# Delta rule and cosine router: chunks of 64 tokens with two sequences to a tile, in place of chunks of 128

## The chip, the cores and the metric

The kernel runs on one core of a Trainium2 chip. TensorE (PE; PEld is its weight load) multiplies, VectorE (DVE), ScalarE (ACT) and GpSimd (POOL) work on what it makes, SyncE (SP) issues most transfers. The metric is the device time of one execution in microseconds, less is better.

## The reference

Four sequences, 8 heads, 768 tokens, head size 48, all in float32. A delta rule makes one output row a token; the rows (3072 of 384) go to a router that picks one of 8 experts by cosine similarity, and each expert is two matrix products with a ReLU between them.

```
k_n = k / (norm(k) + 1e-06)
for t in range(S):
    kt, vt, bt = k_n[:, :, t], v[:, :, t], beta[:, :, t, None]
    y[:, :, t] = einsum('bhd,bhde->bhe', q[:, :, t], state)
    v_old = einsum('bhde,bhd->bhe', state, kt)
    state = state + bt * einsum('bhd,bhe->bhde', kt, vt - v_old)
x = y.transpose(0, 2, 1, 3).reshape(B * S, H * D)
logits = (x / |x|) @ (emb / |emb|).T / tau          # argmax picks the expert, softmax gives the gate
out[mask] = gate_w[mask] * (maximum(x[mask] @ w1[e], 0) @ w2[e])
```

## The kernel before, in words

The tokens of a sequence are cut into chunks (NC = 6 of C = 128). Inside a chunk the loop over tokens becomes linear algebra: with A the strictly triangular part of beta-weighted K K^T, the new values are Z = (I + A)^-1 (V - K S), the outputs Q S + (Q K^T) Z, and the state grows by (beta K)^T Z. A tile holds the 128 tokens of one sequence; heads lie behind each other in the free dimension.

`prep` (L182) normalises K on POOL and DVE. `front` (L201) transposes K, Q and beta K on PE (L207, copied out by ACT, L208), makes K K^T and K Q^T of each head (L215; the 48 rows of a head at partition 0 or 64), masks them (L220 on DVE, L222 and L223 on ACT and POOL) and starts the inverse, W, on POOL (L228, L229). `invert` (L233) doubles the inverted blocks in six levels (`LEVELS` 2 to 64); each level of a group of four heads is four transposes (L240, copied by ACT, L242), four products (L248, masked by DVE, L251) and four more (L257, added by DVE, L260). Two sequences, so four groups, go through a level together. `back` (L262) then does for each sequence K S (L268, R on DVE, L271), the solve (L276, Z on ACT), Q S and the outputs (L284, L287), the state (L299, added by DVE, L303), the transposes of the output (L307) and its logits (L312). `route` (L315) runs once a chunk: small DVE instructions, two small products (L349) and four indirect writes of token numbers to `idmap` by POOL (L362).

The loop (L367) runs over 6 chunks and, in each, over 2 pairs of sequences. The order of the instructions on each engine is made by a scheduler from the program. PSUM has two rings of tiles, `big` (5) and `seq` (3). Behind the loop the second half runs over 31 tiles of 128 routed tokens: fetch of indices, rows and weights, three transposes (L443), 24 products (L453), 8 products (L458), and the result is written by index (L461). A float32 product is two instructions on PE (each row of the trace counts them so), a transpose is one.

Of the kernel before, what the change touches and what calls it, by code (L numbers as in the profile page):

```python
# [15 lines left out]
C = 128  # L16
T = 128
LEVELS = (2, 4, 8, 16, 32, 64)
# [3 lines left out]
def kernel(  # L22
# [37 lines left out]
    def big(shape):  # L60
        return ps.tile(shape, F32, name="big", tag="big", bufs=5)

    def seq(shape):
        return ps.tile(shape, F32, name="seq", tag="seq", bufs=3)
# [6 lines left out]
    half = cpool.tile([128, B, H], F32, name="half")  # L71
    nc.vector.memset(half, 0.5)
    mask_su = cpool.tile([128, 1, 128], F32, name="mask_su")
    nc.gpsimd.memset(mask_su, 1.0)
    nc.gpsimd.affine_select(out=mask_su, in_=mask_su, compare_op=ALU.is_ge, fill=0.0, base=-1,
                            pattern=[[0, 1], [1, 128]], channel_multiplier=-1)
# [28 lines left out]
    xor_i = ac.tile([128, 128], I32, name="xor_i")  # L105
    row_i = ac.tile([128, 128], I32, name="row_i")
    nc.gpsimd.iota(xor_i, pattern=[[1, 128]], base=0, channel_multiplier=0)
    nc.gpsimd.iota(row_i, pattern=[[0, 128]], base=0, channel_multiplier=1)
    nc.vector.tensor_tensor(xor_i, xor_i, row_i, op=ALU.bitwise_xor)
    xor_f = ac.tile([128, 128], F32, name="xor_f")  # L110
    nc.vector.tensor_copy(xor_f, xor_i)
    nmask1 = ac.tile([128, 1, 128], F32, name="nmask1")
    nc.vector.scalar_tensor_tensor(out=nmask1[:, 0, :], in0=xor_f, scalar=1.0, in1=mask_su[:, 0, :],
                                   op0=ALU.is_equal, op1=ALU.mult)
    nc.vector.tensor_scalar_mul(nmask1, nmask1, -1.0)
    nlow = ac.tile([128, 128], F32, name="nlow")
    nc.gpsimd.memset(nlow, -1.0)
    nc.gpsimd.affine_select(out=nlow, in_=nlow, compare_op=ALU.is_ge, fill=0.0, base=-1,
                            pattern=[[-1, 128]], channel_multiplier=1)
    nmask = {}  # L120
    for s in LEVELS:
        m = ac.tile([128, 1, 128], F32, name=f"nmask{s}")
        nc.vector.scalar_tensor_tensor(out=m[:, 0, :], in0=xor_f, scalar=float(s), in1=nlow,
                                       op0=ALU.is_ge, op1=ALU.mult)
        if 2 * s < C:
            nc.vector.scalar_tensor_tensor(out=m[:, 0, :], in0=xor_f, scalar=float(2 * s), in1=m[:, 0, :],
                                           op0=ALU.is_lt, op1=ALU.mult)
        nmask[s] = m


    Qp = []
    for i in range(2):
        t = ac.tile([128, B, H, 64], F32, name=f"Qp{i}")
        nc.gpsimd.memset(t, 0.0)
        Qp.append(t)
    KK = []
    for i in range(6):
        t = ac.tile([128, 2, H, 64], F32, name=f"KK{i}")
        nc.vector.memset(t, 0.0)
        KK.append(t)  # L140
    S_bd = ac.tile([128, B, NP, 2, D], F32, name="S_bd")
    nc.vector.memset(S_bd, 0.0)

    def load(c):
        K4 = io.tile([128, B, H, D], F32, name="K4", tag="K4")
        V4 = io.tile([128, B, H, D], F32, name="V4", tag="V4")
        for b in range(B):
            for dst, src in ((K4[:, b], k), (Qp[c % 2][:, b, :, 0:D], q), (V4[:, b], v)):
                nc.sync.dma_start(out=dst, in_=src[b, :, c * C:(c + 1) * C, :].rearrange("h p d -> p h d"))
        return K4, V4  # L150
# [7 lines left out]
    loaded = load(0)  # L158
# [345 lines left out]
```

## Time and profile before

| | us |
|---|---|
| median of 3 runs | 1604.41 (1603.41 to 1612.71) |
| profiled execution | 1606.1 |
| its span, first to last instruction | 1604.3 |
| PE busy | 1389.4 (87%) |
| DVE, ACT, POOL busy | 561.2, 309.6, 336.1 |
| mean granted clock of TensorE | 0.865 |

The page has the busy time of each engine, the span in 40 slices, the chain that ended last and the costliest groups of instructions. Waits are named by the engine and line that ended them. [...]

### The profile page before, as it was taken

Reading aid. Unit: us, or ns where it says so; the run is one execution under the profiler, and the core shown is the slowest. Engines: PE = TensorE matmul, PEld = TensorE weight load, DVE = VectorE, ACT = ScalarE, POOL = GpSimd, SP = SyncE. Lnnn points to the kernel's source line nnn. Section 1 sums busy time; section 2 is a strip of 40 time slices with the busy share of each in tenths; the row PEclk is TensorE's granted clock in tenths of the full one; section 3 lists DMA queues with packets and bytes.
Section 4 is the critical chain, followed back from the end, with each engine's and each line's share of the span. In section 5 each row is a group of like instructions: output and inputs, shape, how many; then the busy total and the mean of one; then the engine's idle time right before and its main releaser. Section 6 shows DMA issues by size and latency. Waiting matters only on the chain. (4 is left out here: it accounts for less than half of the span.)

```text
span 1604.3 us, 24107 instructions
## 1 busy us (share of the span) xinstructions
PE 1389.4 (87%) x10166; PEld 1275.2 (79%) x10166; DVE 561.2 (35%) x1001; ACT 309.6 (19%) x599; POOL 336.1 (21%) x316
## 2 busy tenths in 40 slices
PE   3698997989879898798988989799892799999997
PEld 2697987979779798797978979699792578878875
DVE  4451644426344263442634435253352001110110
ACT  2122221222212222112221132222220011111110
POOL 7803024030240302203031030400301111111110
PEclk9796978979779797897968999598895799999999
DMA  9100021000210002000010000000001999999991
GB/s 153 21 1 11 1 50 20 1 11 1 53 18 1 11 1 50 1 1 11 1 40 1 1 1 1 20 1 1 1 1 54 356 330 324 317 327 325 330 318 48
DMA packets 132349, 129.04 MB, mean 80 GB/s; under 512 B 82698, under 2 KB 117681, under 8 KB 132242
## 3 DMA queue, kind: packets, MB, share of 16 engines
q1 hardware_dynamic: 127298, 116.55, 24.3%
q0 software_dynamic: 4736, 10.85, 1.9%
q8 instruction: 80, 1.31, 0.3%
q14 instruction: 27, 0.22, 0.0%
q10 hardware_dynamic: 208, 0.11, 0.0%
HBM read 117.91 MB, written 10.95 MB: 80 GB/s over the span
## 5 line engine op out<-in xcount | busy, mean ns | idle before, releaser
L251 DVE TENSOR_TENSOR Pm<-big,nmask 128x512 f32<-128x512 f32 x288 | 198.2, 691 | 308.6 <-PE big L248 308.6
L248 PE MATMUL big<-Ti,LM 128*128 128x128 f32 x2304 | 292.1, 289 | 0.0
L248 PEld LDWEIGHTS big<-Ti,LM 128*128 128x128 f32 x2304 | 287.3, 206 | 0.0
L257 PE MATMUL big<-W,Pm 128*128 128x128 f32 x2304 | 269.5, 275 | 2.6 <-DVE Pm L251 2.6
L257 PEld LDWEIGHTS big<-W,Pm 128*128 128x128 f32 x2304 | 263.1, 192 | 3.2 <-DVE Pm L251 3.2
L242 ACT ACTIVATE Ti<-big 128x512 f32<-128x512 f32 x288 | 152.8, 600 | 562.9 <-PE big L240 562.9
L240 PE MATMUL big<-ident,W 128*128 128x128 f32 x1152 | 157.4, 287 | 111.5 <-POOL W L229 107.2
L240 PEld LDWEIGHTS big<-ident,W 128*128 128x128 f32 x1152 | 134.1, 147 | 126.1 <-POOL W L229 118.3
L260 DVE TENSOR_TENSOR W<-big,W 128x512 f32<-128x512 f32 x288 | 198.8, 692 | 56.4 <-PE big L257 56.2
L453 PE MATMUL big<-xTm,w 128*128 128x128 f32 x1488 | 173.1, 277 | 0.0
L453 PEld LDWEIGHTS big<-xTm,w 128*128 128x128 f32 x1488 | 170.7, 194 | 0.3
L458 PE MATMUL seq<-w,hT 128*128 128x384 f32 x496 | 165.1, 486 | 0.0
L196 POOL TENSOR_TENSOR KK<-KK,betaT 128x384 f32<-128x384 f32 x24 | 19.7, 827 | 594.8 <-PE seq L299 594.8
L458 PEld LDWEIGHTS seq<-w,hT 128*128 128x128 f32 x496 | 91.9, 190 | 57.5
L460 DVE TENSOR_SCALAR y<-seq,xg 128x384 f32<-128x384 f32 x31 | 19.1, 618 | 305.0 <-PE seq L458 305.0
L455 ACT ACTIVATE hT<-big 128x512 f32<-128x512 f32 x62 | 37.0, 598 | 336.4 <-PE big L453 291.3
L215 PE MATMUL big<-KT 48*128 48x256 f32 x384 | 71.1, 487 | 10.1 <-ACT KT L208 10.1
L287 PE MATMUL seq<-Z,LM 128*128 128x48 f32 x384 | 65.8, 341 | 2.3 <-ACT Z L279 2.3
L215 PEld LDWEIGHTS big<-KT 48*128 48x128 f32 x384 | 50.3, 235 | 21.4 <-ACT KT L208 14.8
L287 PEld LDWEIGHTS seq<-Z,LM 128*128 128x128 f32 x384 | 64.7, 262 | 2.9 <-ACT Z L279 2.9
L461 POOL DMA_INDIRECT out_dram<-y,ids x31 | 31.5, 1018 | 163.2 <-DVE y L460 159.8
L228 POOL TENSOR_TENSOR W<-LM,nmask 128x512 f32<-128x512 f32 x48 | 60.7, 1265 | 10.2 <-DVE LM L220 9.2
(131 smaller groups left out, 1026.4 us busy)
## 6 DMA issues: line engine op xcount, KB each, us to landing
w<-in_moe_w_dram SPq DMA_DIRECT2D x62, 1536.0 KB, 9.5
x_dram<-xc SPq DMA_DIRECT2D x6, 770.0 KB, 4.1
K<-in_k_dram SPq DMA_DIRECT2D x24, 192.0 KB, 4.0
V<-in_v_dram SPq DMA_DIRECT2D x24, 192.0 KB, 4.1
Qp<-in_q_dram SPq DMA_DIRECT2D x24, 192.0 KB, 3.1
ids<-idmap SPq DMA_DIRECT2D x31, 0.5 KB, 8.6
xg<-x_dram,ids POOLq DMA_INDIRECT x31, 6.9
out_dram<-y,ids POOLq DMA_INDIRECT x31, 7.1
```

The source lines that it names most:

```text
L215: nc.tensor.matmul(psG[:, i], lhsT=KT[pr, 2 * g + i, 2, :], rhs=KT[pr, 2 * g + i, 0:2, :], start=True, stop=True, skip_group_check=True)
L228: nc.gpsimd.tensor_tensor(W, LM[:, hh, :, 0, :], nmask1.broadcast_to([128, NP, 128]), op=ALU.mult)
L240: nc.tensor.transpose(psI[:, j, :], W[:, j, :], ident)
L242: nc.scalar.activation(Ti, psI, ACT.Copy)
L248: nc.tensor.matmul(psP[:, j, :], lhsT=AT[:, j, :], rhs=Ti[:, j, :], start=True, stop=True, skip_group_check=True)
L251: nc.vector.tensor_tensor(Pm, psP, nmask[s].broadcast_to([128, NP, 128]), op=ALU.mult)
L257: nc.tensor.matmul(psW[:, j, :], lhsT=Pm[:, j, :], rhs=W[:, j, :], start=True, stop=True, skip_group_check=True)
L260: nc.vector.tensor_tensor(Wn, psW, W, op=ALU.add)
L287: nc.tensor.matmul(psY[:, h, :], lhsT=LM[:, h % 2, h // 2, 1, :], rhs=Z[:, h, :], start=(c == 0 and h == 0), stop=True, skip_group_check=True)
L453: nc.tensor.matmul(psH[:, i, :], lhsT=w1[:, j, (f + i) * 128:(f + i + 1) * 128], rhs=xT[:, j, :], start=(j == 0), stop=(j == KC - 1))
L455: nc.scalar.activation(hT[:, f:f + 4, :], psH, ACT.Relu)
L458: nc.tensor.matmul(psO, lhsT=hT[:, f, :], rhs=w2[:, f, :], start=(f == 0), stop=(f == NF - 1))
```

## The change

Chunks are 64 tokens (NC = 12), and a tile holds the 64 tokens of two sequences, one in each half of the partitions (`HALF`); a chunk is therefore two tiles, u = 0 and 1, for the four sequences. Every product of the recurrence is a 64 by 64 tile of TensorE: rows from one half of the partitions, columns to one half. `products`, `of_state`, `state`, `base` and `grow` use all four places of the array in turn, and the two row halves write different PSUM banks; `x_plain`, `x_square`, `solve`, `lower`, `outputs` and `last` use two (both rows and both columns, on a diagonal). The transposes stay 128 by 128.

The inverse starts from blocks of 4 rows, (I + X)(I + X^2) with X the masked A (`x_plain`, `x_square`, `base`), and goes through four levels (4 to 32). It keeps T, the transpose of W, beside W: `grow` makes both from the same operands, so the transposes of the levels are gone, and `lower` multiplies with A masked for each level beforehand on POOL (`AN`, four a tile, with `XT` and `XTI` before them). beta is put into the mask (`MM`) on POOL, so beta K is not transposed. All PSUM tiles share one ring, `bank` (8).

The steps of `front(c+1)` and of `back(c)` alternate in the program, one step of `back` behind each second step of `front`; on PE that order is kept as written, the other engines are scheduled as before. `route` runs once in two chunks. The second half keeps its instructions. The diff, cut to its core (A is the strictly triangular part of LM):

```diff
-C = 128
+C = 64
 T = 128
-LEVELS = (2, 4, 8, 16, 32, 64)
+LEVELS = (4, 8, 16, 32)
...
-        return ps.tile(shape, F32, name="big", tag="big", bufs=5)
...
-        return ps.tile(shape, F32, name="seq", tag="seq", bufs=3)
...
+        return ps.tile(shape, F32, name="bank", tag="bank", bufs=8)
...
+            p, u = slice(b % 2 * C, b % 2 * C + C), b // 2
...
+    HALF = (slice(0, C), slice(C, 2 * C))
+
+    def mm(out, lhsT, rhs, start=True):
+        nc.tensor.matmul(out, lhsT=lhsT, rhs=rhs, start=start, stop=True, skip_group_check=True)
...
+            nc.gpsimd.tensor_tensor(MM[(c * NU + u) % len(MM)], upper.broadcast_to([128, H, C]),
+                                    betaT[:, c, u].unsqueeze(2).broadcast_to([128, H, C]), op=ALU.mult)
...
+    def front(c):
...
+        def transposes():
+            for u in us:
+                kk = KK[(c * NU + u) % len(KK)]
...
+                for i, src in enumerate((kk[:, 0], Qp[c % 2][:, u])):
+                    psT = bank([128, NP, 128])
+                    for j in range(NP):
+                        nc.tensor.transpose(psT[:, j, :], src[:, 2 * j:2 * j + 2, :].rearrange("p h d -> p (h d)"),
+                                            ident)
+                    nc.scalar.activation(KT[u][:, :, i, :], psT, ACT.Copy)
...
+        def products():
+            for u in us:
...
+                psG = [bank([128, NP, 2, C]) for _ in range(2)]
+                for j in range(NP):
+                    for jj in range(2):
+                        pr = slice(jj * C, jj * C + D)
+                        for i in range(2):
+                            mm(psG[jj][HALF[i], j], KT[u][pr, j, 0, HALF[i]], KT[u][pr, j, :, HALF[i]])
...
+                for jj in range(2):
+                    nc.vector.tensor_tensor(LM[u][:, jj], psG[jj],
+                                            mv[:, jj].unsqueeze(2).broadcast_to([128, NP, 2, C]), op=ALU.mult)
...
+                nc.gpsimd.tensor_tensor(XT[u], A, nmask[0].broadcast_to([128, H, C]), op=ALU.mult)
...
+                nc.gpsimd.tensor_tensor(XTI[u], XT[u], id64h, op=ALU.add)
+                for s in LEVELS:
...
+                    nc.gpsimd.tensor_tensor(AN[u, s], A, nmask[s].broadcast_to([128, H, C]), op=ALU.mult)
...
+        def x_plain():
+            for u in us:
+                p = bank([128, H, C])
+                for h in range(H):
+                    for i in range(2):
+                        mm(p[HALF[i], h], XT[u][HALF[i], h], id64[HALF[i], 0])
...
+                nc.scalar.activation(X[u], p, ACT.Copy)
...
+        def x_square():
...
+                        mm(p[HALF[i], h], XT[u][HALF[i], h], X[u][HALF[i], h])
...
+                nc.vector.tensor_tensor(X2[u], p, id64h, op=ALU.add)
...
+        def new_t(u, p):
...
+            nc.scalar.activation(T_[u], p, ACT.Copy)
...
+        def new_w(u, p):
...
+            nc.vector.tensor_copy(W[u], p)
...
+        def base():
...
+                pt, pw = bank([128, H, C]), bank([128, H, C])
+                for h in range(H):
+                    for i in range(2):
+                        mm(pt[HALF[i], h], XTI[u][HALF[i], h], X2[u][HALF[i], h])
+                        mm(pw[HALF[1 - i], h], X2[u][HALF[i], h], XTI[u][HALF[i], h])
+                new_t(u, pt)
+                new_w(u, pw)
...
+        def lower(s):
...
+                        mm(p[HALF[1 - i], h], AN[u, s][HALF[i], h], T_[u][HALF[i], h])
...
+                nc.vector.tensor_tensor(Pm[u], p, id64h, op=ALU.add)
...
+        def grow(s):
...
+                        o = HALF[1 - i]
+                        mm(pw[o, h], Pm[u][o, h], W[u][o, h])
+                        mm(pt[HALF[i], h], W[u][o, h], Pm[u][o, h])
+                new_t(u, pt)
+                new_w(u, pw)
...
+        def last():
...
+                        mm(p[HALF[i], h], Pm[u][o, h], W[u][o, h])
...
+                nc.scalar.activation(W[u], p, ACT.Copy)
...
+        steps = [transposes, products, x_plain, x_square, base]
+        for s in LEVELS[:-1]:
+            steps += [lambda s=s: lower(s), lambda s=s: grow(s)]
+        steps += [lambda: lower(LEVELS[-1]), last]
+        return steps, (KT, LM, W)
...
+        def of_state():
...
+                                mm(p[jj][HALF[i], u, j], KT[u][pr, j, a, HALF[i]], S_all[pr, u, j, i])
...
+                        nc.vector.tensor_tensor(dv, vv, p[jj], op=ALU.subtract)
...
+                        nc.scalar.activation(dv, p[jj], ACT.Copy)
...
+        def solve():
...
+                        mm(p[HALF[i], h], w[HALF[i]], r[HALF[i], u, h])
...
+                nc.scalar.activation(Z[u], p, ACT.Copy)
...
+        def state():
...
+                        mm(p[i][HALF[h % 2], u, h // 2], kb[HALF[i], h], Z[u][HALF[i], h])
+            for i in range(2):
+                nc.vector.tensor_tensor(S_all[:, :, :, i], p[i], S_all[:, :, :, i], op=ALU.add)
...
+        def outputs():
...
+                        mm(p[HALF[i], h], LM[u][HALF[i], h % 2, h // 2, 1], Z[u][HALF[i], h])
...
+                    nc.vector.tensor_tensor(xb, pf, Yq[0][:, u].rearrange("p h d -> p (h d)"), op=ALU.add)
...
+        def x_transposes():
...
+        def logits():
...
+        return [of_state, solve, state, outputs, x_transposes, logits]
...
+    with tc.manual_schedule(engines={mybir.EngineType.PE}):
+        prep(0, loaded[0][0])
+        loaded[1] = load(1)
+        steps, fr = front(0)
+        for f in steps:
+            f()
...
+        for c in range(NC):
...
+            if c + 2 < NC:
+                loaded[c + 2] = load(c + 2)
+            bs = back(c, fr, loaded.pop(c)[1], xc, ssx, lz)
+            if c + 1 < NC:
+                prep(c + 1, loaded[c + 1][0])
+                steps, fr = front(c + 1)
+                for i, f in enumerate(steps):
+                    f()
+                    if i % 2 == 1 and bs:
+                        bs.pop(0)()
+            for f in bs:
+                f()
+            if c % 2 == 1:
+                route(c, xc, ssx, lz)
```

On POOL, before, the front of a pair of sequences has for each of its four groups a select, a masking and an addition of the unit matrix:

```order
L223 AFFINE_SELECT LM<-LM 128x512
L228 TENSOR_TENSOR W<-LM,nmask_111 128x512
L229 TENSOR_TENSOR W<-W,ident 128x512
L223 AFFINE_SELECT LM<-LM 128x512
L194 TENSOR_TENSOR KK_144<-K_1650,rn 128x8x48
L228 TENSOR_TENSOR W<-LM,nmask_111 128x512
L229 TENSOR_TENSOR W<-W,ident 128x512
```

In the change POOL has these rows in `front(5)`, from the scatter of the token numbers that `route(3)` leaves to the first tile's masks (`XT`, `XTI`, `AN`) and on to the second tile's `XT`, the last row:

```order
L490 DMA idmap<-tokid,slot_i 28544x1 x2
L275 TENSOR_TENSOR XT<-LM,nmask_132 128x512
L280 TENSOR_TENSOR AN_4601<-LM,nmask_135 128x512
L277 TENSOR_TENSOR XTI<-XT,id_126 128x512
L280 TENSOR_TENSOR AN_4603<-LM,nmask_138 128x512
L280 TENSOR_TENSOR AN_4605<-LM,nmask_141 128x512
L490 DMA idmap<-tokid,slot_i 28544x1
L280 TENSOR_TENSOR AN_4607<-LM,nmask_144 128x512
L275 TENSOR_TENSOR XT<-LM,nmask_132 128x512
```

So the second tile's `XT` stands behind all six masks of the first, and in odd fronts the two scatters stand ahead of both. In `front(4)`, without scatters, POOL goes on behind the second tile's `XT` like this, up to the norms of a later chunk (`Ksq`, and `rn` to the power one half):

```order
L280 TENSOR_TENSOR AN_3687<-LM,nmask_135 128x512
L277 TENSOR_TENSOR XTI<-XT,id_126 128x512
L280 TENSOR_TENSOR AN_3689<-LM,nmask_138 128x512
L280 TENSOR_TENSOR AN_3691<-LM,nmask_141 128x512
L280 TENSOR_TENSOR AN_3693<-LM,nmask_144 128x512
L238 TENSOR_TENSOR MM_159<-upper,betaT 128x512
L238 TENSOR_TENSOR MM_160<-upper,betaT 128x512
L228 TENSOR_TENSOR Ksq<-K_6367 128x768
L231 TENSOR_TENSOR rn<-rn,half 128x16
```

The norms of a later chunk, which stood between the fronts, now stand behind twelve masks and two `MM`. On DVE, before, a pair of sequences goes through the levels in this order:

```order
L220 TENSOR_TENSOR LM<-big,mask_su 128x512 x4
L251 TENSOR_TENSOR Pm<-big,nmask_117 128x512 x4
L260 TENSOR_TENSOR W<-big,W 128x512 x4
L251 TENSOR_TENSOR Pm<-big,nmask_120 128x512 x4
L260 TENSOR_TENSOR W<-big,W 128x512 x4
```

In the change DVE has this in `front(4)`, from the masked products to the first `lower` (`Pm`) and the state; L230, L232 and L233 are the later chunk's norms:

```order
L271 TENSOR_TENSOR LM<-bank,MM_159 128x512 x2
L271 TENSOR_TENSOR LM<-bank,MM_160 128x512 x2
L377 TENSOR_TENSOR R<-V_1733,bank 128x8x48 x2
L298 TENSOR_TENSOR X_3824<-bank,id_126 128x512
L298 TENSOR_TENSOR X_3843<-bank,id_126 128x512
L230 TENSOR_REDUCE rn<-Ksq 128x16
L306 COPY W<-bank 128x512
L232 TENSOR_SCALAR rn<-rn 128x16
L233 RECIPROCAL rn<-rn 128x16
L306 COPY W<-bank 128x512
L325 TENSOR_TENSOR Pm<-bank,id_126 128x512 x2
L402 TENSOR_TENSOR S_all<-bank,S_all 128x8x48 x2
```

The reduction of POOL's `Ksq`, and two instructions on POOL's `rn`, now stand between the evictions of the inverse: in the fronts 1 to 7, since chunk 11's norms stand in `front(7)`.

## Rows read from the trace of the kernel before

**Rows 1.** The page: the span, and busy time with share and instructions.

```profile
span 1604.3 us, 24107 instructions
...
PE 1389.4 (87%) x10166; PEld 1275.2 (79%) x10166; DVE 561.2 (35%) x1001; ACT 309.6 (19%) x599; POOL 336.1 (21%) x316
```

**Rows 2.** Stretches: length; PE, PEld, DVE, ACT, POOL busy us (count); clock; DMA; GB/s.

```profile
0.00:24.40 24.40, 1.31 (x10) 1.12 (x10) 16.28 (x40) 1.90 (x3) 16.17 (x24) 1.00 1.18 170
24.40:1217.40 1193.00, 1048.19 (x8079) 1002.15 (x8079) 504.98 (x866) 270.64 (x534) 254.49 (x227) 0.84 0.06 13
1217.40:1604.30 386.90, 339.90 (x2080) 271.92 (x2080) 39.90 (x95) 37.05 (x62) 65.40 (x66) 0.94 0.83 283
```

**Rows 3.** Timeline of PE: start us, us, line, tile, count, idle before.

```profile
504.42 3.74 PE L257 MATMUL big<-W,Pm 128*128 128x128 f32 x32
...
510.65 1.91 PE L287 MATMUL seq<-Z,LM 128*128 128x48 f32 x16
512.49 0.67 PE L299 MATMUL seq<-Z,KK 128*64 128x48 f32 x16
...
516.71 3.65 PE L276 MATMUL seq<-R,W 128*128 128x48 f32 x16 [0.65 <-DVE R L271]
...
537.47 2.10 PE L215 MATMUL big<-KT 48*128 48x256 f32 x16 [0.79 <-ACT KT L208]
...
542.53 0.66 PE L240 MATMUL big<-ident,W 128*128 128x128 f32 x4 [2.37 <-POOL W L229]
```

**Rows 4.** Timeline of PE in the second half of the kernel.

```profile
1274.80 5.33 PE L458 MATMUL seq<-w,hT 128*128 128x384 f32 x16
```

**Rows 5.** Instructions of L299: duration ns least/median/most, first and last start.

```profile
L299 PE MATMUL seq<-Z,KK x320: 222/307/343, 117.0 to 1012.3; 128*64 128x48 f32 x160
```

**Rows 6.** Timeline of the 20 ns in which L299 begins.

```profile
512.28 0.28 PE L287 MATMUL seq<-Z,LM 128*128 128x48 f32 x1
512.49 0.14 PEld L299 LDWEIGHTS seq<-Z,KK 128*64 128x64 f32 x2
512.49 0.26 PE L299 MATMUL seq<-Z,KK 128*64 128x48 f32 x2
```

**Rows 7.** Stretches between changes of the granted clock, columns as in rows 2.

```profile
441.50:458.50 17.00, 6.10 (x28) 5.70 (x29) 1.75 (x2) 1.58 (x3) 11.14 (x10) 0.50 0.22 36
458.60:516.50 57.90, 56.89 (x519) 56.33 (x517) 34.62 (x54) 12.28 (x25) 6.29 (x2) 1.00 0.00 1
516.60:533.60 17.00, 16.89 (x89) 16.45 (x91) 1.49 (x5) 3.74 (x8) 1.66 (x2) 0.50 0.06 12
```

**Rows 8.** Groups by line: busy us, mean ns, idle before and its releaser.

```profile
L251 DVE TENSOR_TENSOR Pm<-big,nmask 128x512 f32<-128x512 f32 x288 | 198.2, 691 | 308.6 <-PE big L248 308.6
...
L240 PE MATMUL big<-ident,W 128*128 128x128 f32 x1152 | 157.4, 287 | 111.5 <-POOL W L229 107.2 <-DVE W L260 4.2
L242 ACT ACTIVATE Ti<-big 128x512 f32<-128x512 f32 x288 | 152.8, 600 | 562.9 <-PE big L240 562.9
...
L228 POOL TENSOR_TENSOR W<-LM,nmask 128x512 f32<-128x512 f32 x48 | 60.7, 1265 | 10.2 <-DVE LM L220 9.2
...
L188 POOL TENSOR_TENSOR rn<-rn,half 128x32 f32<-128x32 f32 x6 | 32.7, 5448 | 11.2 <-DVE rn L187 8.3 <-DVE ess L173 2.9
...
L187 DVE TENSOR_REDUCE rn<-Ksq 128x32 f32<-128x1536 f32 x6 | 10.5, 1747 | 10.9 <-POOL Ksq L185 10.9
```

**Rows 9.** Timeline of DVE behind the last product of a level.

```profile
508.19 0.69 DVE L260 TENSOR_TENSOR W<-big,W 128x512 f32<-128x512 f32 x1 [0.20 <-PE big L257]
```

**Rows 10.** Timeline of POOL: scatters of token numbers at the end of the first half.

```profile
1221.32 1.06 POOL L362 DMA_INDIRECT idmap<-tokid,slot_i  x1 [7.72 <-DVE ends L406]
1225.66 0.96 POOL L362 DMA_INDIRECT idmap<-tokid,slot_i  x1 [3.29 <-DMA idmap<-tokid,slot_i]
```

**Rows 11.** Timeline of the start.

```profile
11.11 2.88 POOL L185 TENSOR_TENSOR Ksq<-K 128x1536 f32<-128x1536 f32 x1 [4.02 <-DMA K<-in_k_dram]
...
24.39 1.12 PE L207 MATMUL big<-ident,KK 128*128 128x128 f32 x4 [6.00 <-POOL KK L194]
```

More of the change, by code (lines that the diff above doesn't have):

```diff
@@ L113 @@
[L113 to L119, printed above, removed]
+    prow = ac.tile([128, C], I32, name="prow")
@@ new lines @@
+    nc.gpsimd.iota(prow, pattern=[[0, C]], base=0, channel_multiplier=1)
+    trow = ac.tile([128, C], I32, name="trow")
+    nc.vector.tensor_single_scalar(trow, prow, C - 1, op=ALU.bitwise_and)
+    xor_i = ac.tile([128, C], I32, name="xor_i")
+    nc.gpsimd.iota(xor_i, pattern=[[1, C]], base=0, channel_multiplier=0)
+    col_f = ac.tile([128, C], F32, name="col_f")
+    nc.vector.tensor_copy(col_f, xor_i)
+    nc.vector.tensor_tensor(xor_i, xor_i, trow, op=ALU.bitwise_xor)
+    xor_f = ac.tile([128, C], F32, name="xor_f")
@@ L341, in route @@
         nc.vector.tensor_scalar_add(den, den, 1e-9)
[L342 to L350 removed]
+        nc.vector.reciprocal(gate, den.unsqueeze(2))
@@ L351, in route @@
+        xd = x_dram[0:N, :].rearrange("(u i s) d -> i s u d", i=2, s=S)
+        for o in range(2):
+            t0 = (c - 1 + o) * C
+            for i in range(2):
+                nc.sync.dma_start(xd[i, t0:t0 + C], xc[HALF[i], o])
+        psR = bank([128, 2, G, E])
+        ohf = oh.rearrange("p g e -> p (g e)")
+        for i, w in enumerate((mask_su, ones)):
+            mm(psR[:, i].rearrange("p g e -> p (g e)"), w, ohf)
+        rk = t("rk", [128, 2, G, E])
         nc.vector.tensor_copy(rk, psR)
-        for b in range(B):
-            nc.vector.tensor_tensor(rk[:, 0, b], rk[:, 0, b], run, op=ALU.add)
-            nc.vector.tensor_tensor(run, run, rk[:, 1, b], op=ALU.add)
@@ L355, in route @@
-        nc.vector.tensor_tensor(rk[:, 0], rk[:, 0], base_e.broadcast_to(be), op=ALU.add)
+        for g in range(G):
+            nc.vector.tensor_tensor(rk[:, 0, g], rk[:, 0, g], run, op=ALU.add)
+            nc.vector.tensor_tensor(run, run, rk[:, 1, g], op=ALU.add)
+        nc.vector.tensor_tensor(rk[:, 0], rk[:, 0], base_e.broadcast_to(ge), op=ALU.add)
         nc.vector.tensor_tensor(rk[:, 0], rk[:, 0], oh, op=ALU.mult)
-        slot = t("slot", [128, B])
+        slot = t("slot", [128, G])
@@ L366 @@
[L366 to L384 removed]
+                out=idmap[:, :], out_offset=bass.IndirectOffsetOnAxis(ap=slot_i[:, g:g + 1], axis=0),
```

380 lines of the change are left out of this document (183 added, 197 removed).

## Prediction

> **What bounds the kernel now.** I read the page first: PE is busy for 87% of the span [rows 1]. Three stretches follow [rows 2]: 24.4 us to the first transpose of K, 1193.0 us of recurrence, and 386.9 us from the routing of the last chunk to the end. The change touches the second stretch, a little of the first and none of the third. In the second PE is busy for 1048 of 1193 us at a granted clock of 0.84, DVE for 505, ACT 271, POOL 254; it waits mostly for POOL's start of the inverse, 107 us in all, ahead of L240 [rows 8]. So what is to be priced is PE's instructions, their clock, and who stands in PE's way once they are fewer.
>
> **The price of a product.** Pitches come from the timeline, the last instruction's own length taken off. L257 (128 columns moving, 128-wide weights) has (3.74 - 0.28)/31 = 0.112 us an instruction, and L287 with 48 columns (1.91 - 0.28)/15 = 0.109 [rows 3, 6]: up to 128 columns the width of the weights sets it. L299 has 64-wide weights, in the two column halves of the array by turns: (0.67 - 0.22)/15 = 0.030 [rows 3, 5], a quarter, so half the width counts half and the two halves work side by side; two of its instructions begin within 20 ns although each lasts 222 or more [rows 5, 6]. L215 alternates between two row halves: 2.10/16 = 0.131 for 256 columns against 5.33/16 x 256/384 = 0.222 without halves [rows 3, 4]. Products that use both halvings at once, as the change's, stand in no row. So 64 by 64 in two places costs 30 ns an instruction, and in four places between 15 ns (four side by side) and 30 (two). I take 22, between the ends, since no row is nearer to either.
>
> [...]
>
> **PE's work in one front with its back.** Instructions on the chip are two a product. Two places: `x_plain`, `x_square`, four `lower` and `last` 448, `solve` and `outputs` 128, together 576 x 30 ns = 17.3 us. Four places: `base` and three `grow` 512, `of_state` 128, `state` 64, together 704 x 22 = 15.5 (10.6 to 21.1). `products`, 128 columns, 64 x 42 ns = 2.7 (1.7 to 3.5; the ends are a quarter and a half of 0.323/3). 22 transposes and 12 of the logits at 0.11: 3.7. Sum 39.2 us (33.3 to 45.6), where before a chunk of twice the tokens took 1193/6 = 199.
>
> **What stands in PE's way.** The 512-wide DVE and ACT evictions take 0.69 and 0.60 us [rows 8] and begin 0.2 us behind the pitch's end [rows 3, 9]; a tile's step of 32 instructions at 30 ns is 0.96 us, so the other tile covers an eviction, and I count 1 us a front for what is not covered. DVE's sum is 22 evictions of 0.69, six of 0.55 (three quarters, with a fixed part) and about 4 of small ones, 22.5 us; ACT's is 14. Neither is the bound. POOL's is: masks of 1.265 us each [rows 8], six a tile.
>
> *First wait, `x_plain` of the second tile.* From the front's first transpose: transposes 1.75, last copy and `products` of tile 0 to 3.25, eviction 0.2 + 2 x 0.69, so LM is there at 4.85. POOL makes six masks of tile 0, then XT of tile 1: 4.85 + 7 x 1.265 = 13.7. PE has `products` to 4.6, `of_state` to 7.4, `x_plain` of tile 0 to 8.4: it waits 5.3 us. *Second wait, `grow`(4), in fronts 1 to 7.* DVE holds at the later chunk's norms: POOL finishes its masks at 20.0, two MM 2.5, Ksq at half of 2.88, 1.4; DVE's reduction 0.9 (half of 1.75); POOL's power 2.7 (half of 5.45); two small ones 0.5; then W and Pm 1.4: 29.5 [rows 8, 11]. PE, from 13.7: `x_plain` 1.0, `x_square` 1.9, `solve` 1.9, `base` 2.8, `lower` 1.9, `state` 1.4, to 24.6; it waits 4.9. *Odd fronts from 3 on* (five): two scatters, the second behind the landing of the first, 1221.3 to 1226.6 [rows 10], put XT off by about 4.
>
> Fronts 1 to 7: 39.2 + 5.3 + 4.9 + 1 = 50.4; 8 to 11: 45.5; with 5 x 4: 353 + 182 + 20 = 555 us.
>
> **The clock.** Now a stretch of waits for POOL runs at 0.5 (17 us, PE busy 6.1) and so do 17 us in which PE is full, 16.89, but mostly with 48 or 96 columns under 128-wide weights; the levels run at 1.0 [rows 7]. At 0.5 an instruction takes double (L276: 3.65 us for what L287 does in 1.91 at 1.0 [rows 3]). Those 6.1 us would have been 3 at 1.0; a front has more to do behind its waits, and I take 10 us of work at 0.5 behind each, so 5 us lost; behind the first it is swallowed by the second in fronts 1 to 7, so one loss a front: 11 x 5 = 55. Ends: none, and twice that.
>
> **Sum.** Start: Ksq begins at 11.1 as now, and Ksq 1.4, MM 2.5, power 2.7, small ones 0.5 and KK 0.9 follow, plus gaps: 20. Front 0 has no steps of back beside it, but POOL sets it: 29.5 + 16 + 1 + 4 = 50. Fronts 1 to 11: 610. The last back, all its evictions bare, with the routing: 14. Together 694. Third stretch 386.9. 694 + 387 = 1081, and 1.8 us lie outside the span (1606.1 - 1604.3; that execution is 1.7 above the median): **1083 us**, a fall of 523.
>
> Ends of this case: four places at 15 ns and no clock loss, fronts 512, the rest 78: 979. Four places at 30 ns and double clock loss, fronts 706, the rest 94: 1189.
>
> **Rivals.**
> *The clock stays at 0.5 through the recurrence.* For it: half of the array is idle in 576 of 1378 instructions, and PE full with 48 columns was no protection [rows 7]. Against: here columns move in nearly all the time of a weight load, as in L257. All PE work doubles, 78.4 us, POOL's waits vanish behind it, 80 a front: 880 + 20 + 62 + 20 + 389 = 1371 (1240 to 1510 by the two prices of four places).
> *POOL is quicker or overlaps better* (shorter waits than computed, no clock loss): below 979, not below 930 with half of the waits gone as well.
> *The evictions stand bare.* If the two tiles of a step don't cover each other, each of 19 steps a front adds about 0.9 us (0.2 + 0.69): 17 us, less the 1 counted, 16 x 11 = 176, or 1259. For it: order on DVE and ACT, which carry more than 40 instructions a front. Against: in the levels before, PE waited for DVE 4.2 us in all at L240 [rows 8], and DVE's 22.5 us of 50 leave room. [...]
> *Slower: products in different quarters do not overlap.* One mechanism: an instruction in another quarter waits for the end of the one before, 222 ns [rows 5] in place of 30. Then 1344 x 0.222 = 298 us a front and about 4000 us. It decides from 70 ns an instruction on: (1217 - 20 - 14)/12 = 98.6 us a front, less 4.7 for the rest, over 1344. For it: no row has both halvings at once. Against: each alone overlaps [rows 3, 5, 6]. [...]
>
> **Chances.** The sum's case 0.63, half clock throughout 0.20, bare evictions 0.05, quicker 0.05, no overlap 0.05, something that eats the gain to within 1% 0.02. The range 960 to 1330 holds the first, the bare evictions, most of the quicker one and about the lower third of the half clock: 0.8. Faster by over 1%, about what a measurement of this kernel can tell from no change, 0.94; within 1% 0.01; slower 0.05.
>
> **What would show it.** In the new trace: about 18,450 PE instructions; `x_plain` and `lower` at 30 ns, `grow` and `of_state` between 15 and 30; idle PE ahead of the second tile's `x_plain`, released by POOL XT, 5 to 9 us in all 12 fronts; idle PE ahead of the first `grow`, released by DVE behind L232, in eight of them and in no later one; a granted clock of 0.5 behind those waits and 1.0 in the later levels. The prediction falls if 64 by 64 products keep the clock at 0.5, if four places go no faster than one, or if POOL's masks take another time than 1.265 us beside a busier DVE.

## The result, and the profile after

The changed kernel takes **1072.74 us** (median of 4 runs, 1066.16 to 1074.46); the kernel before took 1603.91 us beside it. The ratio is 0.668, 95% interval 0.664 to 0.672. The forecast was 1083 us, range 960 to 1330. The profiled execution took 1073.31 us. How it splits is close to the forecast too, but one term of the sum was wrong, and another that was missing made up for it.

The page of the changed kernel, first its span and the engines' busy time (compare [rows 1]):

```profile
span 1071.5 us, 39767 instructions
...
PE 820.4 (77%) x18454; PEld 729.8 (68%) x18454; DVE 312.7 (29%) x664; ACT 197.0 (18%) x381; POOL 388.9 (36%) x350
```

The three stretches (columns as in [rows 2]): start, recurrence, and the rest from the end of the last routing's products.

```profile
0.00:20.30 20.30, 1.30 (x9) 1.10 (x9) 14.63 (x49) 1.90 (x3) 13.15 (x25) 1.00 0.66 117
20.30:682.60 662.30, 479.35 (x16368) 456.80 (x16368) 258.17 (x520) 158.06 (x316) 310.29 (x260) 0.86 0.15 28
682.60:1071.50 388.90, 339.74 (x2077) 271.89 (x2077) 39.90 (x95) 37.02 (x62) 65.46 (x66) 0.93 0.83 282
```

The recurrence fell from 1193.0 to 662.3 us, the start by 4 us, and the rest rose by 2. TensorE now has 16368 instructions in the recurrence instead of 8079 (18454 in all, about 18,450 forecast), and is busy there for 479 us instead of 1048. What TensorE waited for (us in total, times, longest):

```profile
PE bank L223 <- POOL XT L275: 102.5, 19, 7.3
PE bank L223 <- issue: 55.1, 66, 2.2
PE bank L578 <- DMA xg<-x_dram,ids: 39.4, 2, 30.9
PE bank L223 <- DVE Pm L325: 21.2, 8, 5.5
```

The first and the last are the two waits of the forecast. The third lies in the rest. The second, "issue", is time in which TensorE waits for nothing that the profile shows: 55 us in 66 pieces, and the forecast has no such term.

Groups by line on GpSimd and VectorE (columns as in [rows 8]):

```profile
L280 POOL TENSOR_TENSOR AN<-LM,nmask 128x512 f32<-128x512 f32 x96 | 120.0, 1269 | 0.3
L231 POOL TENSOR_TENSOR rn<-rn,half 128x16 f32<-128x16 f32 x12 | 35.0, 2916 | 20.5 <-DVE rn L230 20.5
...
L306 DVE COPY W<-bank 128x512 f32<-128x512 f32 x96 | 65.0, 685 | 65.9 <-PE bank L223 65.9
L325 DVE TENSOR_TENSOR Pm<-bank,id 128x512 f32<-128x512 f32 x96 | 65.5, 689 | 48.8 <-PE bank L223 48.8
```

A mask takes 1.269 us and an eviction 0.69, as priced from [rows 8]; the power takes 2.9, where 2.7 was priced.

### What the idle "issue" is

Two readings of the trace of the changed kernel tell it. First, TensorE's timeline in a busy part of front 8, only the rows with an idle stretch ahead of them (in brackets):

```profile
480.62 0.84 PE L223 MATMUL bank<-Z,KK 64*64 64x48 f32 x42 [0.68 <-issue]
...
484.37 0.21 PE L223 MATMUL bank<-Pm,W 64*64 64x64 f32 x1 [1.61 <-issue]
...
488.11 1.42 PE L223 MATMUL bank<-Z,LM 64*64 64x48 f32 x41 [0.37 <-issue]
```

They come 3.75 and 3.74 us apart, in three different steps of the program. Second, the stretches from one to the next:

```profile
480.60:484.36 3.76, 2.14 (x128) 2.00 (x128) 1.69 (x3) 0.60 (x1) 1.62 (x2) 1.00 0.02 4
484.36:488.10 3.74, 3.37 (x128) 3.21 (x127) 2.07 (x3) 0.60 (x1) 0.00 (x0) 1.00 0.02 4
488.10:491.84 3.74, 2.77 (x128) 2.64 (x128) 1.12 (x2) 1.72 (x5) 0.87 (x1) 1.00 0.02 4
```

Each holds 128 matmul instructions with their weight loads (127 or 128 of these fall into the stretch), whatever the work: 256 instructions. Where they need 2.1 us, TensorE idles for the rest. Counted through the whole recurrence, 58 of the 66 pieces, 52.2 of the 55.1 us, stand in such steps of 128 matmul instructions (at times 127) from one another; the other eight, 2.9 us in all, come in pairs near 185, 294, 403 and 511 us. The page's list of DMA queues has a queue of the kind "instruction"; here are its lines for the changed kernel and for the experiment grow_twice below, which has 4608 matmul instructions and 4608 weight loads more:

```profile
q8 instruction: 145, 2.38, 1.0%
```

```profile
q8 instruction: 181, 2.97, 1.1%
```

9216 instructions more cost 36 packets more: 256 in each, 16 KB (2.38 MB over 145). At 256 the changed kernel's 145 packets hold 37,120 instructions, and its trace has 36,908 matmuls and weight loads. I read from this that TensorE's program itself is brought in by DMA, 256 instructions at a time, and that the blocks come at a pace of their own, the 3.74 to 3.76 us above. Where one idle piece follows the next by one block (23 times in this trace), 3.41 to 4.03 us lie between them, 3.75 in the middle: about **29.2 ns for a matmul instruction with its load**, 27 to 31 in single blocks. A packet itself takes about 1.2 us (1.0% of 16 engines' span, over 145); what fills the rest of the 3.75 us is not shown. I call this the feed. In the expectations below "128 products" are 128 such matmul instructions; a product of the kernel is two of them.

### The profile page after: what moved, and what is told of

It is laid out like the page before. It is cut to its first block, busy times and chain, and to the rows that moved or that the text cites. A ratio compares the mean times of both kernels' runs of the same rounds, so it can differ in the third digit from the quotient of the medians.

```text
span 1071.5 us, 39767 instructions
## 1 busy us (share of the span) xinstructions
PE 820.4 (77%) x18454; PEld 729.8 (68%) x18454; DVE 312.7 (29%) x664; ACT 197.0 (18%) x381; POOL 388.9 (36%) x350
## 3 DMA queue, kind: packets, MB, share of 16 engines
q8 instruction: 145, 2.38, 1.0%
## 5 line engine op out<-in xcount | busy, mean ns | idle before, releaser
L588 PE MATMUL bank<-xTm,w 128*128 128x128 f32 x1488 | 173.5, 277 | 0.0
L588 PEld LDWEIGHTS bank<-xTm,w 128*128 128x128 f32 x1488 | 171.1, 194 | 0.3
L593 PE MATMUL bank<-w,hT 128*128 128x384 f32 x496 | 165.1, 486 | 0.0
L223 PE MATMUL bank<-W,Pm 64*64 64x64 f32 x3072 | 115.6, 231 | 27.8 <-DVE Pm L325 21.2
L593 PEld LDWEIGHTS bank<-w,hT 128*128 128x128 f32 x496 | 91.9, 190 | 57.5
L223 PEld LDWEIGHTS bank<-W,Pm 64*64 64x64 f32 x3072 | 105.6, 145 | 33.6 <-DVE Pm L325 23.9
L223 PE MATMUL bank<-id,XT 64*64 64x64 f32 x768 | 42.0, 287 | 103.8 <-POOL XT L275 102.5
L280 POOL TENSOR_TENSOR AN<-LM,nmask 128x512 f32<-128x512 f32 x96 | 120.0, 1269 | 0.3
L223 PE MATMUL bank<-Pm,W 64*64 64x64 f32 x2304 | 89.9, 233 | 7.9 <-issue 7.5
L223 PEld LDWEIGHTS bank<-Pm,W 64*64 64x64 f32 x2304 | 81.9, 145 | 8.4 <-issue 8.4
L325 DVE TENSOR_TENSOR Pm<-bank,id 128x512 f32<-128x512 f32 x96 | 65.5, 689 | 48.8 <-PE bank L223 48.8
```

Of the source, the lines that this page charges most:

```text
L223: nc.tensor.matmul(out, lhsT=lhsT, rhs=rhs, start=start, stop=True, skip_group_check=True)
L280: nc.gpsimd.tensor_tensor(AN[u, s], A, nmask[s].broadcast_to([128, H, C]), op=ALU.mult)
L325: nc.vector.tensor_tensor(Pm[u], p, id64h, op=ALU.add)
L588: nc.tensor.matmul(psH[:, i, :], lhsT=w1[:, j, (f + i) * 128:(f + i + 1) * 128], rhs=xT[:, j, :], start=(j == 0), stop=(j == KC - 1))
L593: nc.tensor.matmul(psO, lhsT=hT[:, f, :], rhs=w2[:, f, :], start=(f == 0), stop=(f == NF - 1))
```

## The experiments

All start from the changed kernel. Differences between runs, as "42 us less", are differences of their ratios times 1603.9, since each was measured beside other runs of the kernel before; the changed kernel's 0.6676 is 1071 on that scale.

### Two places by turns in place of four (two_places)

```diff
                 for h in range(H):
                     for i in range(2):
                         o = HALF[1 - i]
-                        mm(pw[o, h], Pm[u][o, h], W[u][o, h])
                         mm(pt[HALF[i], h], W[u][o, h], Pm[u][o, h])
+                for h in range(H):
+                    for i in range(2):
+                        o = HALF[1 - i]
+                        mm(pw[o, h], Pm[u][o, h], W[u][o, h])
```

(`base` in the same way.)

> The changed kernel with the products of base and of the three grow steps written in another order: per tile first the 16 products of T (two places of the array by turns), then the 16 of W (the two other places), where the change takes all four places by turns. Same products, same count. Theory A, the feed: in the changed kernel's trace TensorE stands idle for nothing shown 66 times, 55.1 us, and in a long busy stretch these gaps come at every 128th product (starts at 480.62, 484.37, 488.11, 491.85 us), so 128 products (256 instructions with their weight loads) take 3.74 us, 29 ns each, however fast the places are. Two places cost 30 ns anyway, so only the products that run from what was fetched during a wait lose: some 100 to 150 products a front by 15 ns, 2 us: 1073 + 12 x 2 = 1097 at most, 1073 to 1097, and the idle time for nothing shown falls from 55 us to under 15. Theory B, the places: the pitch of 14.5 ns in four places is what the time rests on: 512 products a front by 15 ns, 8 us, 12 fronts: 1165 (1150 to 1180), with the idle time for nothing shown no smaller than now.

Measured: 1076.03 us, ratio 0.6666 (0.6647 to 0.6685): the same as the changed kernel. Its recurrence:

```profile
19.60:685.00 665.40, 516.21 (x16368) 497.10 (x16368) 258.12 (x521) 157.50 (x316) 310.38 (x260) 0.88 0.15 28
```

TensorE is busy for 37 us more (516 against 479), and idles for 34 us less on "issue" (21.0 against 55.1; I had expected less than 15). Theory A: working four places by turns instead of two is worth nothing to the time here, because the feed gives an instruction only every 29.2 ns, and two places keep that pace.

### Products of one place after the other (one_place)

```diff
-                for h in range(H):
-                    for i in range(2):
+                for i in range(2):
+                    for h in range(H):
                         mm(p[HALF[i], h], XT[u][HALF[i], h], X[u][HALF[i], h])
```

(so in all steps with 64 by 64 products, and `products`, `of_state`, `solve`, `state` by place too)

> The changed kernel with every loop of 64 by 64 products ordered by place: all products of one place of the array (8 in a run, 16 instructions) before those of the next, in the front's steps and in those of the back. Same products, same count. Theory A, work in different places overlaps only between neighbours in the program: one place takes 60 ns an instruction (two places by turns take 30), so a front's 1280 instructions of this kind take 77 us where they take 40 now, and with its transposes 81: 20 + 12 x 81 + 20 + 390 = 1400 (1300 to 1450); idle time for nothing shown near zero. Theory B, the engine itself takes products for different places out of order or out of several queues (the kernel before, L215, ran two row halves interleaved although the program has four of one and then four of the other): 1073 to 1110.

Measured: 1807.04 us, ratio 1.118 (1.114 to 1.122). The same instructions in another order cost two thirds more, and the kernel is **slower than before the change**. Both theories missed the size. A stretch of one_place, and its timeline where `x_plain` ends and `x_square` begins (the program has all of `bank<-id,XT` ahead of `bank<-X,XT`):

```profile
128.50:473.20 344.70, 339.76 (x3921) 336.79 (x3920) 62.07 (x116) 38.66 (x75) 75.19 (x63) 0.50 0.06 12
```

```profile
256.22 0.36 PE L223 MATMUL bank<-X,XT 64*64 64x64 f32 x1
256.32 0.31 PE L223 MATMUL bank<-id,XT 64*64 64x64 f32 x1
256.38 0.31 PE L223 MATMUL bank<-X,XT 64*64 64x64 f32 x1
256.43 0.31 PE L223 MATMUL bank<-id,XT 64*64 64x64 f32 x1
256.49 0.31 PE L223 MATMUL bank<-X,XT 64*64 64x64 f32 x1
256.54 0.31 PE L223 MATMUL bank<-id,XT 64*64 64x64 f32 x1
256.60 5.29 PE L223 MATMUL bank<-X,XT 64*64 64x64 f32 x58
```

TensorE is busy for 99% of these 345 us, and the granted clock is 0.50: an instruction takes 344.7/3921 = 88 ns. Inside a run the starts are 107 ns apart. Half of these, 44 and 53 ns, is my estimate for the full clock, after L276 and L287 [rows 3]; so theory A was near with 60 for a run with no partner; it did not think of the clock. Where the place changes, three instructions of the old run alternate with three of the new one, and the new run's first begins 0.10 us ahead of the old run's last three.

### Runs of two and of four products (runs2, runs4)

```diff
-                for h in range(H):
-                    for i in range(2):
-                        mm(p[HALF[i], h], XT[u][HALF[i], h], X[u][HALF[i], h])
+                for h0 in range(0, H, R):
+                    for i in range(2):
+                        for h in range(h0, h0 + R):
+                            mm(p[HALF[i], h], XT[u][HALF[i], h], X[u][HALF[i], h])
```

(R is 2 or 4; `base`, `grow` also with T's products ahead of W's; `of_state`, `state`, `products` as they were)

> The changed kernel with runs of 2 products (4 instructions) in one place of the array before the next place, in all steps of the inverse, in solve and outputs; between the present order (1 product) and the kernel with runs of 8. In the trace with runs of 8, inside a run an instruction starts every 107 ns at the half clock, and only where a run ends do the last three instructions alternate with the first three of the next (60 and 47 ns). Theory A, the engine begins about three instructions ahead of what waits: of 4 in a run all find a partner, the pitch stays at the feed's 29 ns: 1076 (1068 to 1092). Theory B, the overlap exists only where program neighbours differ in place: of 4 instructions two overlap, the pitch is 0.75 x 53 = 40 ns at full clock: 1280 x 11 ns x 12 = 170 more: 1245, and with the clock at half far above.

> The same with runs of 4 products (8 instructions). Theory A, three instructions ahead: of 8 in a run three at either end find a partner and two stand alone, (2 + 6/2) x 53 / 8 = 33 ns at full clock, 4 ns above the feed's 29: 1076 + 1280 x 4 ns x 12 = 1137 (1090 to 1160) if the clock stays at 1.0 as in the changed kernel; if the clock falls to half, as it did with runs of 8 although TensorE was busy for 95% of the span, 66 ns: 20 + 12 x (84 + 7) + 404 = 1520 (1400 to 1550). Theory B, only neighbours: 7 alone of 8, 50 ns at full clock, 1400; at half clock 1800.

Measured: runs2 1079.85 us, ratio 0.6679 (0.6658 to 0.6701), no difference from the changed kernel; runs4 1156.07 us, ratio 0.7149 (0.7125 to 0.7174), 76 us more. Ten full microseconds of runs4:

```profile
490.00:500.00 10.00, 10.00 (x259) 9.77 (x258) 3.46 (x5) 2.34 (x5) 0.00 (x0) 1.00 0.01 3
```

10.0/259 = 39 ns an instruction at a granted clock of 1.0 (33 expected): slower than the feed's 29.2, so here TensorE, busy for all of the 10.00 us, sets the pace. Theory A in both, runs4 near the upper end of its range. Both times fit theory A's count, that an instruction finds a partner up to three instructions on, as the six that alternate in one_place's rows do. And the clock was 1.0 in these 10 us with runs of 8 instructions where it was 0.50 in one_place's 345 us with runs of 16. One_place also ordered `of_state`, `state` and `products` by place, which runs4 left as they were, so that the length of the runs alone makes this difference is not shown.

### Each grow product twice (grow_twice)

```diff
-                        mm(pw[o, h], Pm[u][o, h], W[u][o, h])
-                        mm(pt[HALF[i], h], W[u][o, h], Pm[u][o, h])
+                        for _ in range(2):
+                            mm(pw[o, h], Pm[u][o, h], W[u][o, h])
+                            mm(pt[HALF[i], h], W[u][o, h], Pm[u][o, h])
```

> The changed kernel with each product of the three grow steps issued twice in succession, into the same place: 384 instructions more a front, 4608 in all, that add nothing to the result. Theory A, the feed: 256 instructions with their weight loads come in 3.74 us, 29.2 ns for a product's instruction: 4608 x 29.2 ns = 135 us more where the feed binds, less what TensorE holds ready after its waits, 20 to 35 us: 1073 + 100 to 135 = 1173 to 1208, with idle time for nothing shown rising by 40 to 65 us. Theory B, the places: 14.5 ns each in four places, 67 us more: 1140 (1130 to 1150), idle time for nothing shown as now.

Measured: 1200.32 us, ratio 0.7459 (0.7433 to 0.7484), 126 us more: 27 ns for each of the 4608 instructions, near the feed's 29.2 and far from the places' 14.5. Idle time on "issue" rose from 55.1 to 101.9 us. Theory A.

### XT of both tiles first (xt_first)

```diff
-                nc.gpsimd.tensor_tensor(XT[u], A, nmask[0].broadcast_to([128, H, C]), op=ALU.mult)
...
+                last_xt = nc.gpsimd.tensor_tensor(XT[u], A, nmask[0].broadcast_to([128, H, C]), op=ALU.mult)
+            with tc.issue_after(last_xt.ins):
+                for u in us:
+                    XTI[u] = wk.tile([128, H, C], F32, name="XTI", tag="XTI", bufs=2)
+                    nc.gpsimd.tensor_tensor(XTI[u], XT[u], id64h, op=ALU.add)
                 for s in LEVELS:
...
+                    for u in us:
...
+                        nc.gpsimd.tensor_tensor(AN[u, s], A, nmask[s].broadcast_to([128, H, C]), op=ALU.mult)
```

(`issue_after` makes GpSimd take what it encloses behind the last XT)

> The changed kernel with GpSimd told to make XT of both tiles before XTI and the four masks AN of either; all instructions the same. It stands there as XT of tile 0, one MM, XT of tile 1, then the rest; the scatters of the routing stay where the scheduler puts them, two of them still ahead of XT in every second front. Theory A, GpSimd's order of masks makes the first wait (102.5 us in 19 waits for XT): XT of tile 1 comes five masks, 6 us, earlier, and the wait is left only behind scatters (5 fronts by some 4 to 6 us): 70 to 80 us go; of this the feed of instructions (128 products in 3.74 us) takes back 2 to 3.7 us a front, since it is during that wait that it gets ahead, 24 to 44 us, and the clock, which falls to half in that wait, gives 10 to 40 us: 1073 - 75 + 35 - 25 = about 1010 (985 to 1040). Theory B, the feed alone sets the pace and the wait only lies where it has to catch up: 1050 to 1073. Theory C, AN of tile 0 made later delays lower of the first level by as much as is gained: 1060 to 1080, with waits for AN in place of those for XT.

Measured: 1036.57 us, ratio 0.6417 (0.6399 to 0.6435), 42 us less, at the upper edge of theory A. Its waits:

```profile
PE bank L223 <- DVE Pm L329: 56.4, 11, 9.1
PE bank L223 <- issue: 55.6, 66, 3.1
...
PE bank L223 <- POOL XT L275: 38.6, 15, 6.2
```

64 us of the wait for XT went, and 35 of them came back in the second wait (21.2 to 56.4): TensorE reaches the first `grow` earlier, but the norms that hold VectorE end no earlier. I had reckoned with the feed as what takes back, and not with this. The feed took nothing back ("issue" 55.6 after 55.1); TensorE's mean granted clock was 0.91 after 0.89. No wait for AN came (theory C).

### The norms off GpSimd (norms_act), and both edits (both)

```diff
-        nc.gpsimd.tensor_tensor(Ksq, K4, K4, op=ALU.mult)
+        nc.scalar.activation(Ksq, K4, ACT.Square)
...
-        nc.gpsimd.tensor_tensor(out=rn, in0=rn, in1=half, op=ALU.pow)
+        nc.scalar.activation(rn, rn, ACT.Sqrt)
```

> The changed kernel with the norms of K off GpSimd: the squares (Ksq) and the square root (rn) are made on ScalarE, the reduction stays on VectorE; GpSimd keeps MM and both products for KK. Theory A: the second wait of the changed kernel (TensorE for Pm, 21.2 us in 8 waits) is VectorE held at rn behind GpSimd's power of 2.9 us; with the power gone VectorE waits for ScalarE at most 1 us, so 15 to 21 us go, with up to 2 us a front for the clock behind it: 1035 to 1058. The first wait, for XT, keeps its 100 us. Theory B: behind that wait TensorE is held by the feed of instructions (128 products in 3.74 us) all the same, so that the wait goes and idle time for nothing shown takes its place: 1065 to 1073.

Measured: 1052.50 us, ratio 0.6514 (0.6494 to 0.6533), 26 us less. The wait for Pm fell from 21.2 to 0.5 us, that for XT rose from 102.5 to 109.3, "issue" rose from 55.1 to 61.9. Theory A. Some 3 us of it are the start, which has the same chain: the first transpose of K begins at 17.5 us in place of 20.3.

> The two earlier edits together: XT of both tiles made first on GpSimd, and the norms of K with square and root on ScalarE. Theory A, the two waits follow each other: with XT first alone TensorE came earlier to the first grow and waited there longer, 56.4 us in 11 waits for Pm instead of 21.2 in 8, since the norms had not come earlier; with both edits that wait goes as well, and half of it comes back as idle time for the feed of instructions: 1036.6 - 56 + 25 = 1005 (990 to 1018). Theory B, the two edits are worth only their own sums, 36 and 20 us: 1016, and with a feed that takes more, 1018 to 1032.

Measured: 1004.69 us, ratio 0.6245 (0.6226 to 0.6265), 69 us less than the changed kernel. On the scale of ratios the two edits alone are worth 42 and 26, so this time does not tell A from B. The waits speak for A: Pm 0.2 us where xt_first had 56.4. But what came back is not the feed alone, as I had it: "issue" rose from 55.6 to 67.0, and the wait for XT from 38.6 to 58.0. The next run shows what that waits for.

### The scatters behind the masks (both_scat)

In an odd front of the changed kernel GpSimd's timeline ahead of the first XT is this:

```profile
293.73 1.06 POOL L490 DMA_INDIRECT idmap<-tokid,slot_i  x1 [1.86 <-DVE slot_i L488]
300.39 0.97 POOL L490 DMA_INDIRECT idmap<-tokid,slot_i  x1 [5.61 <-DMA idmap<-tokid,slot_i]
301.38 1.27 POOL L275 TENSOR_TENSOR XT<-LM,nmask 128x512 f32<-128x512 f32 x1
```

The second scatter waits 5.6 us for the landing of the first, and XT stands behind it. both_scat adds to both:

```diff
-            nc.gpsimd.indirect_dma_start(
+            late.append(lambda g=g: nc.gpsimd.indirect_dma_start(
...
+            with tc.issue_after(masked[0].ins):
+                while late:
+                    late.pop(0)()
```

(`masked` holds the last AN of the odd front)

> As the kernel with both edits, and the four scatters of a routing made to stand behind the masks of the odd front instead of two ahead of XT and one ahead of XTI. Theory A: what is left of the first wait in the kernel with XT first (38.6 us in 15 waits, the longest 6.2) is the landing of a scatter, 5.4 us, in five fronts; another 3 us of XTI in the same fronts: 20 to 40 us less than the kernel with both edits, 965 to 990, and the waits for XT at most 10 us in all. Theory B: the scatters then hold MM and the products for KK of the next chunk behind four landings (4 x 6.5 = 26 us), and the wait moves to the transposes of K: no gain, 995 to 1015, with waits for KK.

Measured: **977.74 us**, ratio 0.6057 (0.6021 to 0.6094), 30 us less than both and 99 less than the change. Theory A. This is the fastest version found. Its waits, and its recurrence:

```profile
PE bank L223 <- issue: 86.2, 85, 3.7
...
PE bank L223 <- POOL XT L277: 7.8, 11, 1.9
```

```profile
17.60:590.60 573.00, 466.36 (x16368) 441.30 (x16368) 256.53 (x520) 176.66 (x345) 261.93 (x237) 0.94 0.17 33
```

The wait for XT is gone, and the feed is the largest wait left: 16368 x 29.2 ns = 478 of the 573 us. By this estimate the next gain would have to come from fewer instructions; no run tried it.

### Blocks of 2 rows (rows2)

```diff
-LEVELS = (4, 8, 16, 32)
+LEVELS = (2, 4, 8, 16, 32)
...
-        steps = [transposes, products, x_plain, x_square, base]
+        steps = [transposes, products, x_plain]
```

(`x_plain` then gives T = X + I, W is XTI, and the first level's `lower` writes into the half it reads)

> One part of the change undone: the inverse starts from blocks of 2 rows instead of 4. x_square and base go (192 instructions on TensorE a front), lower and grow of level 2 come (192); GpSimd makes one mask more for each tile (7 instead of 6), VectorE one eviction more and ScalarE one less. Theory A, GpSimd's row of masks sets the first wait: XT of tile 1 comes one mask, 1.27 us, later in 12 fronts: 15 us more, and the norms behind the masks come 2.5 us later, up to 2.5 us a front in the second wait of 8 fronts: 1073 + 15 to 35 = 1088 to 1108. Theory B, the number of products or of levels sets the time: the same number of instructions, one level more with its evictions: 1070 to 1082.

Measured: 1096.97 us, ratio 0.6822 (0.6804 to 0.6839), 23 us more with the same number of instructions on TensorE. The wait for XT rose from 102.5 to 120.8 us, that for Pm from 21.2 to 30.9, 28 us together. Theory A: what the blocks of 4 rows save is mainly one mask for each tile on GpSimd; the part of VectorE's one eviction more in the wait for Pm is not shown apart.

## Why the prediction was right, point by point

**The sum.** Forecast and measured, per front where it says so (the 12 fronts with the last back and routing are the recurrence):

| Term | forecast, us | measured, us |
|---|---|---|
| start | 20 | 20.3 |
| TensorE's work at full clock, a front | 39.2 | 35.7 or more |
| half clock, a front | 5 | at most 4.3 |
| the feed, a front | none | 55.1/12 = 4.6 |
| wait for XT, scatters included, a front | 5.3 + 20/12 = 7.0 | 102.5/12 = 8.5 |
| wait behind the norms, a front | 4.9 x 8/12 = 3.3 | 21.2/12 = 1.8 |
| evictions not covered, a front | 1 | in no row of the waits |
| recurrence | 50 + 610 + 14 = 674 | 662.3 |
| third stretch | 386.9 | 388.9 |

That the time came out within 1% is in part luck: work and feed are off by nearly the same amount in opposite directions, and so are the two waits. (The fall of 523 was counted from the profiled execution; from the median it is 521.)

**Two places, 30 ns.** Right: in two_places two places keep step with a feed of 29.2 ns, and in the changed kernel `solve` takes (1.96 - 0.28)/61 = 27.5 ns:

```profile
473.08 1.96 PE L223 MATMUL bank<-R,W 64*64 64x48 f32 x62
```

**Four places, 22 ns: the step that failed.** I took the middle of 15 and 30 since no row was nearer to either; the price is neither. While instructions are at hand, four start within 20 ns, and the next four some 60 ns after the first of these, 14.5 to 15 ns each, as in `base` here:

```profile
477.22 0.22 PE L223 MATMUL bank<-XTI,X 64*64 64x64 f32 x1
477.23 0.22 PE L223 MATMUL bank<-X,XTI 64*64 64x64 f32 x1
477.23 0.22 PE L223 MATMUL bank<-XTI,X 64*64 64x64 f32 x1
477.24 0.22 PE L223 MATMUL bank<-X,XTI 64*64 64x64 f32 x1
477.28 0.22 PE L223 MATMUL bank<-XTI,X 64*64 64x64 f32 x1
```

At 14.5 the 704 instructions take 10.2 us instead of 15.5, 5.3 less; the feed then takes back 4.6. So 22 gave nearly the right sum by luck, for a reason that is not the one I wrote down, and as the two nearly cancel, the time could not show it: two_places and grow_twice did.

**First wait.** The mechanism is shown by xt_first, rows2 and both_scat. In front 4 XT of the second tile is the seventh mask, and TensorE waits for it 6.2 us, where 5.3 was worked out:

```profile
250.24 1.27 POOL L275 TENSOR_TENSOR XT<-LM,nmask 128x512 f32<-128x512 f32 x1
```

```profile
251.57 1.97 PE L223 MATMUL bank<-id,XT 64*64 64x64 f32 x32 [6.18 <-POOL XT L275]
```

The odd fronts from 3 on were put at 4 us more; front 5 waits 12.0 us, front 4 6.2, so 5.8.

**Second wait.** The cause is right, and norms_act shows it; where the wait comes, and its size, are not. I had forecast 4.9 us once in each of the fronts 0 to 7. The trace has eight waits too, but that is chance: four in front 0 (9.9 us in all; the norms of four chunks run beside it), one in each of the fronts 1, 2, 4 and 6 (1.5 to 3.9 us), and none in 3, 5 and 7. In front 4, VectorE at the norms, then Pm, then TensorE:

```profile
265.07 0.79 DVE L232 TENSOR_SCALAR rn<-rn 128x16 f32<-128x16 f32 x1 [2.43 <-POOL rn L231]
...
266.61 1.27 DVE L325 TENSOR_TENSOR Pm<-bank,id 128x512 f32<-128x512 f32 x2
```

```profile
267.34 0.27 PE L223 MATMUL bank<-W,Pm 64*64 64x64 f32 x1 [1.49 <-DVE Pm L325]
```

In front 5 VectorE makes both first Pm ahead of the wait for the power, and so in 3 and 7; I had taken the order of front 4 for all of them:

```profile
323.30 0.69 DVE L325 TENSOR_TENSOR Pm<-bank,id 128x512 f32<-128x512 f32 x1 [2.66 <-PE bank L223]
...
324.77 0.68 DVE L325 TENSOR_TENSOR Pm<-bank,id 128x512 f32<-128x512 f32 x1
327.90 0.81 DVE L232 TENSOR_SCALAR rn<-rn 128x16 f32<-128x16 f32 x1 [2.45 <-POOL rn L231]
```

In the fronts that have it, TensorE came later to it than worked out, being held by XT and by the feed; xt_first, where it comes earlier, has 56 us of this wait.

**Clock.** In the main as forecast: 0.50 around the waits, 1.0 in most of the later levels; but five of the stretches at half clock, 3.4 us each, have TensorE busy throughout. The 21 stretches at half clock in the recurrence sum to this:

```profile
sum 187.80, PE 102.84 PEld 101.50 DVE 31.92 ACT 20.91 POOL 146.97; mean PE 4.90 PEld 4.83 DVE 1.52 ACT 1.00 POOL 7.00
```

TensorE is busy for 102.8 us in them; estimated at half of that for the full clock, after L276 and L287 [rows 3], at most 51 us are lost, 4.3 a front (5 forecast). It is less where the feed would have held the pace anyway.

**The rivals.** Bare evictions did not come: no wait for an eviction stands in the recurrence's list but Pm behind the norms, and 0.3 us for T. Half clock throughout did not come in this order of the products (0.86 in the recurrence). It did in one_place, for most of the recurrence (0.56 in the mean), though there TensorE is busy for 1384.7 of its 1403.8 us; it did not in two_places, where `base` and `grow` too have two places by turns (0.88 in the recurrence). What in one_place's order brings it the runs do not separate. POOL was not quicker than priced: a mask took 1.269 us. No overlap between places decides, I wrote, from 70 ns an instruction on; one_place has 88 and is slower than before, on the side that was named, at 1807 us and not at 4000: inside a run an instruction begins 107 ns behind the one before, though that one lasts 311 there, at a clock of 0.50.

## What to carry to other kernels

Where small products run in several places of the array, write neighbours in the program for different places, at most a few instructions apart: here runs of 4 instructions in one place cost nothing, runs of 8 cost 76 us, and that order alone, with the clock that came with it, was worth some 720 us (ratio 1.118 against 0.668). Here the feed gave a matmul instruction every 29.2 ns, and four places at 14.5 gained nothing over two: near that price, count instructions and not columns. Idle time of a busy engine that comes at every 128th matmul instruction was the mark of it (58 of 66 pieces). When a wait is removed, look at which chain ends next (here XT, then the norms, then scatters, then the feed), and price the edits together.

## What I had not expected of the hardware

- The feed of instructions: 256 in 3.74 us, 36 packets more for 9216 instructions more. In the fastest version two blocks beside scatters (which begin at 366.31 and 371.20 us) took 5.20 and 5.10 us (the first holds 127 matmul instructions). That scatters slow the feed was not tried:

```profile
364.00:369.20 5.20, 3.19 (x127) 2.87 (x127) 2.15 (x4) 1.19 (x2) 0.99 (x1) 1.00 0.04 3
369.20:374.30 5.10, 3.31 (x128) 3.17 (x128) 1.81 (x3) 1.23 (x4) 0.96 (x1) 1.00 0.04 3
```

- A TensorE that is busy for 99% of 345 us was granted 0.50 of its clock when its products ran in one place at a time (16 instructions each). In runs4, with runs of 8, it was granted 1.0 in the 10 us shown above, and 0.89 from 20 to 760 us, waits included.
- In one_place, matmul instructions for another place begin ahead of up to three older ones: at a change of place (256.22 to 256.54 us) six alternate, and these starts are not in program order.
